# Seven of eight tiles first, decays behind the results, weight sums around the scan: four edits to a scan and feed-forward kernel

## Chip, cores and metric

The kernel runs on one NeuronCore of a Trainium2 chip. The metric is device time of one execution in microseconds (us). Five engines run their own instruction streams in order: TensorE (PE, with its weight loads listed as PEld), VectorE (DVE), ScalarE (ACT), GpSimd (POOL) and SyncE (SP), which here issues every DMA. Matrix results land in PSUM, which the tile names `h`, `even`, `odd`, `oa`, `ob` (in `out_units`), `cb`, `y` and `t_ps` stand for.

## What is computed

The first half is a chunked selective scan (Mamba-2 style) over 4 batches, 8 heads, 768 positions; its output, as a matrix of 3072 tokens by 256, goes through a feed-forward layer with 2048 hidden units and a hard-swish.

```python
# scan, per chunk: cum = cumsum(log a)
L = exp(cum[i] - cum[j]) * (i >= j)
y = ((C @ B.T) * L) @ x + (C @ state) * exp(cum)
state = exp(sum(log a)) * state + (B * exp(cum[-1] - cum)).T @ x
# feed-forward on y as (3072, 256)
h = y @ w_in                       # 256 -> 2048
g = h * clip(h + 3, 0, 6) / 6
out = g @ w_out                    # 2048 -> 256
```

## The kernel before

**Blocks.** The sequence is cut in six chunks of 128 positions. Block k is chunk k of all four batches, 512 tokens, and the loop over k computes its feed-forward layer while the scan of chunk c = k + 1 and the decays of chunk k + 2 (`ahead`) are woven in between. Block 0 uses plain products (`mlp_in`, `first_out`) and, during them, still decodes the weights, which arrive as 64-bit numbers.

**First product, blocks 1 to 5.** It is a Strassen-like product (seven half products for eight) in eight steps s = 0 to 7, each giving two hidden tiles, `even` (g tile 2s) and `odd` (2s + 1). A step's parts are `early`, `lead` (of the step after), `last` (of the step before) and `middle`. DVE and ACT copy partial sums into `up`, DVE adds them (L516, L517), ACT takes the ramp (`ramp`, L524), DVE clamps and multiplies (`times_ramp`, L530). In step 7 the ramp of `even` is taken in two halves of 256 columns: the first half before `middle`, the second behind the first unit of the second product.

**Second product, blocks 1 to 5.** `out_units` yields 14 times, one unit of 8 tiles (16 matmuls in the trace, L599) at a time, into four slots of the PSUM banks `oa` and `ob`; it too is of Strassen form. `g_sums` makes its sums of g on POOL (L586), and `weight_sums` and `in_weight_sums` make the sums of the weights on DVE (L568, L472), once, in block 0 (the last one in block 1). Three DVE steps (`u`, `res`, `res`; L630 to L633) then put a half of the result together, and two stores write it.

**The scan.** `turn` transposes B and C of a chunk (PE L343; ACT `bT` L347; DVE `cT` L359 and `csT` L365). `scores` makes C times B (PE `cb` L376), and DVE multiplies the decays by it (`L`, L384). `mix` makes y and the new state (PE `y` L400, L409, L417), `keep` copies them out (ACT `yT` L432, DVE `state` L435, L440). `rows` loads the decays of a chunk (four DMAs into `L`, L247, and eight into `eto`, L253), `conceal` masks them on POOL (L303), `decay` takes their exponent on ACT (L312).

**What sets the order.** The order is written out by hand: each engine runs its instructions in the order in which the program issues them, and the (i, b) cases of block 0 and the step and unit numbers of the later blocks say where the scan's parts go. Buffers matter in two places: `up` and block 0's result tile `ob` (L546, stored by L547) share one tag with two buffers, and `t_ps`, `oa` and `ob` of `out_units` share two PSUM banks.

```python
parts_of[k, s] = up = ffn.tile([P, 2, 2 * P], FP32, name="up", tag="ob", bufs=2)
ob = ffn.tile([P, 2, DM], FP32, name="ob", bufs=2)
```

Of the kernel before, what the change touches and what calls it, by code (L numbers as in the profile page):

```python
# [8 lines left out]
FP32 = mybir.dt.float32  # L9
# [3 lines left out]
AF = mybir.ActivationFunctionType  # L13
ALU = mybir.AluOpType
# [6 lines left out]
def kernel(  # L21
# [23 lines left out]
    nc = tc.nc  # L45
    P = 128
# [3 lines left out]
    NC = S // P  # L50
    TB = NB * P
# [11 lines left out]
    ffn = ctx.enter_context(tc.tile_pool(name="ffn", bufs=1))  # L63
# [39 lines left out]
    def load_w(i):  # L103
# [24 lines left out]
        out=hide, in_=hide, pattern=[[1, P]], compare_op=ALU.is_ge, fill=-1e5, base=0,  # L128
# [9 lines left out]
    half = const.tile([P, 1], FP32, name="half")  # L138
# [304 lines left out]
    gTs, outs = {}, {}  # L443
# [16 lines left out]
    NJ = NF // 2  # L460
# [58 lines left out]
    def last(k, s):  # L519
        half_product(evens[k, s], 1, in_sums[4][s], y_half(k, 1, 1))  # L520

    def ramp(k, f, h, sl=slice(0, TB)):

        nc.scalar.activation(  # L524
            gTs[k][:, f, sl], h.rearrange("p r i -> p (r i)")[:, sl], AF.Relu, bias=half,
            scale=1.0 / 6.0)

    def times_ramp(k, f, h, sl=slice(0, TB)):
        g = gTs[k][:, f, sl]
        nc.vector.scalar_tensor_tensor(  # L530
            out=g, in0=g, scalar=1.0, in1=h.rearrange("p r i -> p (r i)")[:, sl],
            op0=ALU.min, op1=ALU.mult)

    def first_out(b, i):

# [19 lines left out]
    wsums = {}  # L555
# [32 lines left out]
    def out_units(k):  # L588


        def quarter(e, r, t):
            return g_quarter(k, e, r)[:, :, t * P:(t + 1) * P]

        def total(n, t):
            return gsums[k][n][:, :, t * P:(t + 1) * P]

        def unit(bank, slot, lhs, rhs):
            for j in range(NJ):
                nc.tensor.matmul(  # L599
                    out=bank[:, slot], lhsT=lhs[:, j], rhs=rhs[:, j],  # L600
                    start=(j == 0), stop=(j == NJ - 1), skip_group_check=True)

        for t in range(2):
            oa = ps_o.tile([P, 4, P], FP32, name="oa", tag="o")
            if t == 0:
                unit(oa, 0, quarter(0, 0, 0), w4[:, 0, 0])
                yield
                unit(oa, 3, quarter(0, 0, 1), w4[:, 0, 0])
                yield
            unit(oa, 1, quarter(1, 0, t), w4[:, 1, 0])  # L610
            if t == 0:
                x1 = ffn.tile([P, 2, P], FP32, name="x1")
                nc.scalar.copy(out=x1, in_=oa[:, 0:4:3])
            yield
            ob = ps_o.tile([P, 4, P], FP32, name="ob", tag="o")
            unit(ob, 3, quarter(1, 1, t), wsums[4])
            yield
            unit(oa, 2, total(2, t), wsums[2])
            res = ffn.tile([P, 5, P], FP32, name="res", bufs=2)
            nc.vector.tensor_tensor(  # L620
                out=res[:, 0:5:4], in0=oa[:, 1:3],
                in1=x1[:, t:t + 1].to_broadcast([P, 2, P]), op=ALU.add)
            yield
            unit(ob, 2, total(4, t), w4[:, 1, 1])
            yield
            unit(ob, 0, total(1, t), wsums[1])
            yield
            unit(ob, 1, quarter(0, 1, t), wsums[3])
            u = ffn.tile([P, 2, P], FP32, name="u", bufs=2)
            nc.vector.tensor_tensor(  # L630
                out=u, in0=ob[:, 0:2], in1=res[:, 4:5].to_broadcast([P, 2, P]), op=ALU.add)
            nc.vector.tensor_tensor(out=res[:, 1:3], in0=ob[:, 2:4], in1=u, op=ALU.add)
            nc.vector.tensor_tensor(out=res[:, 3], in0=ob[:, 0], in1=u[:, 1], op=ALU.add)  # L633
            for r in range(2):
                r0 = (t + 2 * r) * S + k * P
                nc.sync.dma_start(
                    out=out[r0:r0 + P, :],
                    in_=res[:, 2 * r:2 * r + 2].rearrange("p m c -> p (m c)"))
            yield

    def rows(c):
        for b in range(NB):
            load_decay(c, b)
        load_eto(c)
# [96 lines left out]
    for k in range(NC):  # L741
        gTs[k] = ffn.tile([P, NF, TB], FP32, name="gT")
        c, ahead = k + 1, k + 2
        if k == 0:
            for f in range(NF):
                mlp_in(k, f)
                for i in weave.get(f, []):
                    weights(i, 1)
            load(ahead)
            weights(NP + 1, 1)  # L750
            weights(NP + 3, 1)
            weights(NP + 2, 3)
            sums, sums_in = weight_sums(), in_weight_sums()
            for i in range(NP):
                for b in range(NB):
                    first_out(b, i)
                    if (i, b) == (0, 0):
                        weights(NP + 3, 1)
                        weights(NP + 2, 1)
                        weights(NP + 3, 3)  # L760
                        rows(ahead)
                    elif (i, b) == (1, 0):
                        for _ in sums_in:
                            pass
                    elif (i, b) == (2, 0):
                        turn(c, 0)
                        turn(c, 1)
                        for b_ in range(NB):
                            conceal(ahead, b_)
                    elif (i, b) == (2, 1):  # L770
                        scores(c, (0, 1))
                    elif (i, b) == (2, 2):
                        decay_ends(ahead, 0)
                        next(sums)
                        next(sums)
                    elif (i, b) == (2, 3):
                        results(c, 0)
                        scores(c, (2, 3))
                        decay_ends(ahead, 1)
                    elif (i, b) == (3, 0):  # L780
                        next(sums)
                        decay_ends(ahead, 2)
                    elif (i, b) == (3, 1):
                        results(c, 1)
                        sum_y(c)
                        rows(ahead + 1)
                        decay_ends(ahead, 3)
                        from_start(ahead)
                    elif (i, b) == (3, 2):
                        lead(c, 0)  # L790
            continue
        for s in range(NJ):
            early(k, s)
            if s == 0:
                if ahead < NC:
                    load(ahead)
                if c < NC:
                    carry(c)
            if s < NJ - 1:
                lead(k, s + 1)  # L800
            elif c < NC:
                turn(c, 1)
            if s:
                last(k, s - 1)
                ramp(k, 2 * s - 2, evens[k, s - 1])
            if s == NJ - 1:
                sl = slice(0, 2 * P)
                ramp(k, 2 * s, evens[k, s], sl)
                times_ramp(k, 2 * s, evens[k, s], sl)
            middle(k, s)  # L810
            if s:
                times_ramp(k, 2 * s - 2, evens[k, s - 1])
            ramp(k, 2 * s + 1, odds[k, s])
            times_ramp(k, 2 * s + 1, odds[k, s])
            if s in (1, 3) and ahead < NC:
                conceal(ahead, s - 1)
                conceal(ahead, s)
            if s == 4 and c < NC:
                turn(c, 0)
            if s in (2, 4, 6):  # L820
                g_sums(k, s - 2)
        for i, _ in enumerate(out_units(k)):
            if i == 0:
                s, sl = NJ - 1, slice(2 * P, TB)
# [52 lines left out]
```

## Time and profile before

| | us |
|---|---|
| median of 3 runs (390.64 to 394.83) | 391.48 |
| the profiled execution | 390.89 |
| its span | 389.2 |
| PE busy | 365.7 (94%) |
| PE weight loads | 310.7 (80%) |
| DVE busy | 229.1 (59%) |
| ACT busy | 188.2 (48%) |
| POOL busy | 132.6 (34%) |
| one block of 1 to 4, start to start | about 58 |

The profile is of one execution. A row of the timeline reads: start, length, engine, line, instruction, tile written <- tiles read, sizes, count; in brackets the idle time before it and what ended that. "SPq" is the queue of SyncE. Line numbers are those of the kernel before. Matmuls are pipelined, so that the length of a group of them is a little more than the time until the next group starts. A `half_product` is x2 and a unit x16 in the trace.

### The profile page before, as it was taken

What the parts mean: (1) busy time and instruction counts of PE and PEld (TensorE: products, weight loads), DVE (VectorE), ACT (ScalarE), POOL (GpSimd) and SP (SyncE); (2) the same over time, 40 slices, a digit from 0 to 9 for tenths busy, and PEclk for the clock granted to TensorE, in tenths of its full rate; (3) what the DMA queues carried; (4) which work ended last, traced back from release to release, by engine and by line L of the source; (5) the groups of instructions that cost most, each with busy time, mean ns of one, the idle gap of its engine ahead of it and who ended that gap; (6) DMA issues with size and microseconds to landing.
All of it is one profiled execution on the core that took longest, in us unless ns stands there. A gap on an engine that the chain in (4) does not pass through costs nothing.

```text
span 389.2 us, 7304 instructions
## 1 busy us (share of the span) xinstructions
PE 365.7 (94%) x2916; PEld 310.7 (80%) x2916; DVE 229.1 (59%) x454; ACT 188.2 (48%) x405; POOL 132.6 (34%) x131
## 2 busy tenths in 40 slices
PE   7889999899499999999999999999998999998995
PEld 4554458678388899987899987999987999987995
DVE  7768999874278733288533388533388523387211
ACT  5759786347267291277290277290276100366100
POOL 1100000533039822149812049800047800058700
PEclk9999999989999999999999999999999999999999
DMA  9949979506880005590004590000000000000000
GB/s 162 237 175 102 306 175 127 198 2 199 140 68 1 2 3 172 148 89 0 2 3 183 139 87 0 2 2 29 29 0 2 2 2 29 27 2 0 3 27 29
DMA packets 86403, 28.18 MB, mean 72 GB/s; under 512 B 75425, under 2 KB 81217, under 8 KB 86369
## 3 DMA queue, kind: packets, MB, share of 16 engines
q1 hardware_dynamic: 86368, 27.71, 35.9%
q8 instruction: 23, 0.38, 0.4%
q14 instruction: 12, 0.09, 0.1%
HBM read 24.48 MB, written 3.23 MB: 71 GB/s over the span
## 4 chain that ended last, share of the span: by engine, by line
PE 68%; DVE 12%; DMA 8%; ACT 7%; SPq 3%; issue 1%; DVEq 0%; ACTq 0%
PE ob L599 19%; PE oa L599 14%; PE even L490 12%; PE odd L490 9%; DMA L<-cum_d 5%; PE cb L376 4%; DVE gT L530 3%; PE y L409 3%; ACT gT L524 2%; PE o L541 2%; DVE odd L517 2%; PE y L400 2%; DVE up L504 1%; SPq L85 1%; DMA raw<-in_moe_w_in_dram 1%
## 5 line engine op out<-in xcount | busy, mean ns | idle before, releaser
L586 POOL TENSOR_TENSOR s<-gT 128x512 f32<-128x512 f32 x20 | 26.3, 1315 | 121.0 <-DVE gT L530 121.0
L490 PE MATMUL even<-ts,w_sum 128*128 128x256 f32 x160 | 48.6, 385 | 6.5 <-DVE gT L530 6.5
L524 ACT ACTIVATE gT<-odd,half 128x512 f32<-128x512 f32 x40 | 27.5, 687 | 46.5 <-DVE odd L517 46.5
L503 ACT COPY even<-odd 128x512 f32<-128x512 f32 x40 | 23.0, 575 | 42.9 <-PE odd L490 40.9
L490 PE MATMUL odd<-yT,w_in 128*128 128x256 f32 x160 | 41.1, 379 | 0.0
L490 PEld LDWEIGHTS even<-ts,w_sum 128*128 128x128 f32 x160 | 30.3, 192 | 12.5 <-DVE gT L530 8.5
L599 PEld LDWEIGHTS oa<-w_out,gT 128*128 128x128 f32 x320 | 38.2, 192 | 2.3 <-issue 1.5
L599 PE MATMUL oa<-w_out,gT 128*128 128x128 f32 x320 | 39.8, 278 | 0.0
L312 ACT ACTIVATE L<-L,cum_n 128x128 f32<-128x128 f32 x128 | 38.4, 392 | 2.9 <-POOL L L303 2.9
L504 DVE COPY up<-odd 128x256 f32<-128x256 f32 x40 | 16.9, 423 | 38.6 <-ACT even L503 29.2
L599 PE MATMUL ob<-t,gT 128*128 128x128 f32 x320 | 39.0, 275 | 0.0
L599 PEld LDWEIGHTS ob<-t,gT 128*128 128x128 f32 x320 | 37.6, 192 | 0.2
L599 PE MATMUL ob<-w_out,s 128*128 128x128 f32 x320 | 37.8, 276 | 0.0
L599 PEld LDWEIGHTS ob<-w_out,s 128*128 128x128 f32 x320 | 36.5, 192 | 1.3 <-issue 1.3
L384 DVE TENSOR_TENSOR L<-L,cb 128x512 f32<-128x512 f32 (+1 forms) x56 | 30.3, 605 | 10.9 <-PE cb L376 10.9
L530 DVE SCALAR_TENSOR_TENSOR gT<-gT,odd 128x512 f32<-128x512 f32 x40 | 27.5, 687 | 10.0 <-ACT gT L524 10.0
L490 PEld LDWEIGHTS odd<-yT,w_in 128*128 128x128 f32 x160 | 30.1, 190 | 3.9
L524 ACT ACTIVATE gT<-even,half 128x512 f32<-128x512 f32 (+1 forms) x45 | 28.6, 649 | 5.5 <-PE even L490 5.5
L530 DVE SCALAR_TENSOR_TENSOR gT<-gT,even 128x512 f32<-128x512 f32 (+1 forms) x45 | 27.9, 619 | 5.0 <-ACT gT L524 5.0
L541 PE MATMUL o<-w_out,gT 128*128 128x256 f32 x128 | 30.6, 397 | 0.0
L490 PE MATMUL even<-yT,w_sum 128*128 128x256 f32 x80 | 24.6, 389 | 5.7 <-DVE odd L517 5.7
L541 PEld LDWEIGHTS o<-w_out,gT 128*128 128x128 f32 x128 | 25.1, 199 | 4.8 <-issue 0.9
(105 smaller groups left out, 616.6 us busy)
## 6 DMA issues: line engine op xcount, KB each, us to landing
L<-cum_d SPq DMA_DIRECT2D x16, 512.0 KB, 6.1
raw<-in_moe_w_in_dram SPq DMA_DIRECT2D x4, 1024.0 KB, 8.5
raw<-in_moe_w_out_dram SPq DMA_DIRECT2D x4, 1024.0 KB, 7.2
xt<-in_x_dram SPq DMA_DIRECT2D x6, 512.0 KB, 8.6
out_dram<-res SPq DMA_DIRECT2D x20, 128.0 KB, 1.8
bc<-in_C_dram SPq DMA_DIRECT2D x6, 256.0 KB, 5.7
bc<-in_B_dram SPq DMA_DIRECT2D x6, 256.0 KB, 8.1
eto<-cum_d SPq DMA_DIRECT2D x40, 32.0 KB, 5.0
```

The costliest lines, as they stand in the source:

```text
L312: nc.scalar.activation(L[:, h], L[:, h], AF.Exp, bias=cum_n[:, c, g:g + 1])
L376: nc.tensor.matmul(out=cbs[q][:, b % 2].rearrange("j h i -> j (h i)"), lhsT=bT[rows, b % 2], rhs=cT[rows, b % 2].rearrange("n t i -> n (t ...
L384: nc.vector.tensor_tensor(out=L[:, :, hs], in0=L[:, :, hs], in1=cbs[q][:, in_pair], op=ALU.mult)
L409: nc.tensor.matmul(out=y_ps[u][32 * q:32 * q + 32, b % 2], lhsT=xt[:, b * NH + h], rhs=L[:, h], start=(c == 0), stop=True, tile_position=( ...
L490: nc.tensor.matmul(out=bank[:, r], lhsT=lhsT, rhs=rhs, start=start, stop=True, skip_group_check=True)
L503: nc.scalar.copy(out=even, in_=odd[:, 1:2].to_broadcast([P, 2, 2 * P]))
L504: nc.vector.tensor_copy(out=up[:, 1], in_=odd[:, 0])
L524: nc.scalar.activation(gTs[k][:, f, sl], h.rearrange("p r i -> p (r i)")[:, sl], AF.Relu, bias=half, scale=1.0 / 6.0)
L530: nc.vector.scalar_tensor_tensor(out=g, in0=g, scalar=1.0, in1=h.rearrange("p r i -> p (r i)")[:, sl], op0=ALU.min, op1=ALU.mult)
L541: nc.tensor.matmul(out=o[:, b % 2], lhsT=gTs[0][:, f, b * P:(b + 1) * P], rhs=w_out[:, f], start=(f == 0 and b % 2 == 0), stop=True, skip_ ...
L586: nc.gpsimd.tensor_tensor(out=o, in0=p_, in1=q_, op=op)
L599: nc.tensor.matmul(out=bank[:, slot], lhsT=lhs[:, j], rhs=rhs[:, j], start=(j == 0), stop=(j == NJ - 1), skip_group_check=True)
```

## The change

It has four parts, all of them in the order or the slicing of the work; the number of matmuls is the same.

1. **Block 0's stores.** `rows(ahead + 1)` moves from the case (3, 1) to behind block 0's loop, so that SP issues the two stores of `ob` before the twelve decay loads of chunk 3.
2. **Weight sums of the first product.** `in_weight_sums` yields after four of its eight sums; the first four stay at (1, 0), the other four move to (2, 1), behind the first `scores` of the scan.
3. **Start of the second product.** The first two units run seven of their eight tiles, and the eighth tile of both (g tile 14) follows behind the third unit; the ramp of g tile 14 is taken whole, in `out_units`' first pause, instead of in halves. The turns of the scan go behind steps 3 and 5 instead of behind step 4 and into step 7; the first `scores` goes one unit later.
4. **The last sum.** For the second half of a block's result, `u` and one `res` step are done one unit earlier, and the last unit goes to a slot of `oa`, so that one step of 256 columns is left behind it.

```diff
-        def unit(bank, slot, lhs, rhs):
-            for j in range(NJ):
+        def unit(bank, slot, lhs, rhs, js=range(NJ), clear=False):
+            for j in js:
...
-                    start=(j == 0), stop=(j == NJ - 1), skip_group_check=True)
+                    start=(clear and j == 0), stop=True, skip_group_check=True)
...
-                unit(oa, 0, quarter(0, 0, 0), w4[:, 0, 0])
+                most, rest = range(NJ - 1), range(NJ - 1, NJ)
+                unit(oa, 0, quarter(0, 0, 0), w4[:, 0, 0], most, clear=True)
                 yield
-                unit(oa, 3, quarter(0, 0, 1), w4[:, 0, 0])
+                unit(oa, 3, quarter(0, 0, 1), w4[:, 0, 0], most)
                 yield
-            unit(oa, 1, quarter(1, 0, t), w4[:, 1, 0])
+            unit(oa, 1, quarter(1, 0, t), w4[:, 1, 0], clear=(t == 1))
             if t == 0:
+                unit(oa, 0, quarter(0, 0, 0), w4[:, 0, 0], rest)
+                unit(oa, 3, quarter(0, 0, 1), w4[:, 0, 0], rest)
...
-            unit(ob, 3, quarter(1, 1, t), wsums[4])
+            unit(ob, 3 - 3 * t, quarter(1, 1, t), wsums[4], clear=True)
...
-            unit(ob, 0, total(1, t), wsums[1])
+            unit(ob, 3 * t, total(1, t), wsums[1])
+            u = ffn.tile([P, 2, P], FP32, name="u", bufs=2)
+            u2 = res[:, 4:5].to_broadcast([P, 2, P])
+            if t:
+                nc.vector.tensor_tensor(out=u, in0=ob[:, 0:4:3], in1=u2, op=ALU.add)
+                nc.vector.tensor_tensor(out=res[:, 1], in0=ob[:, 2], in1=u[:, 1], op=ALU.add)
             yield
-            unit(ob, 1, quarter(0, 1, t), wsums[3])
...
+            if t:
+                unit(oa, 0, quarter(0, 1, t), wsums[3], clear=True)
+                nc.vector.tensor_tensor(
+                    out=res[:, 2:4], in0=oa[:, 0:1].to_broadcast([P, 2, P]), in1=u, op=ALU.add)
+            else:
+                unit(ob, 1, quarter(0, 1, t), wsums[3])
...
                     elif (i, b) == (1, 0):
-                        for _ in sums_in:
-                            pass
+                        next(sums_in)
...
                     elif (i, b) == (2, 1):
                         scores(c, (0, 1))
+                        next(sums_in)
...
                         sum_y(c)
-                        rows(ahead + 1)
...
+            rows(ahead + 1)
             continue
...
-            elif c < NC:
-                turn(c, 1)
...
-            if s == NJ - 1:
-                sl = slice(0, 2 * P)
-                ramp(k, 2 * s, evens[k, s], sl)
-                times_ramp(k, 2 * s, evens[k, s], sl)
...
-            if s == 4 and c < NC:
-                turn(c, 0)
+            if s in (3, 5) and c < NC:
+                turn(c, s // 4)
...
-                ramp(k, 2 * s, evens[k, s], sl)
-                times_ramp(k, 2 * s, evens[k, s], sl)
+                ramp(k, 2 * s, evens[k, s])
+                times_ramp(k, 2 * s, evens[k, s])
...
-                if i in (1, 4):
+                if i in (2, 4):
```

SP, from the first decay loads of the loop on: `L` and `eto` are the decays that `rows` loads, `out_dram<-ob` are block 0's two stores, `bc` and `xt` the inputs of chunk 3. Before:

```order
L247 DMA L<-cum_d 128x1024 x4
L253 DMA eto<-cum_d 16x4x128 x8
L547 DMA out_dram<-ob 128x2x256
L247 DMA L<-cum_d 128x1024 x4
L253 DMA eto<-cum_d 16x4x128 x8
L547 DMA out_dram<-ob 128x2x256
L85 DMA bc<-in_C_dram 128x32x16
```

And with the change:

```order
L247 DMA L<-cum_d 128x1024 x4
L253 DMA eto<-cum_d 16x4x128 x8
L546 DMA out_dram<-ob 128x2x256 x2
L247 DMA L<-cum_d 128x1024 x4
L253 DMA eto<-cum_d 16x4x128 x8
L85 DMA bc<-in_C_dram 128x32x16
```

The second store has moved ahead of the twelve decay loads of chunk 3. DVE, in block 0 around the scan of chunk 1 (`w_sum` and `w_in` are the weight sums of the first product, `t` those of the second). Before:

```order
L472 TENSOR_TENSOR w_in<-w_in 128x4x128
L472 TENSOR_TENSOR w_sum<-w_in 128x512
L472 TENSOR_TENSOR w_sum<-w_sum,w_in 128x512
L472 TENSOR_TENSOR w_sum<-w_in,w_sum 128x512
L472 TENSOR_TENSOR w_in<-w_in 128x4x128
L365 TENSOR_TENSOR csT<-t_ps,eto 128x256 x2
L384 TENSOR_TENSOR L<-L,cb 128x2x256 x4
```

And with the change:

```order
L472 TENSOR_TENSOR w_in<-w_in 128x4x128
L365 TENSOR_TENSOR csT<-t_ps,eto 128x256 x2
L384 TENSOR_TENSOR L<-L,cb 128x2x256 x4
L472 TENSOR_TENSOR w_sum<-w_in 128x512
L472 TENSOR_TENSOR w_sum<-w_sum,w_in 128x512
L472 TENSOR_TENSOR w_sum<-w_in,w_sum 128x512
L472 TENSOR_TENSOR w_in<-w_in 128x4x128
```

Six instructions of the scan stand ahead of the second four sums instead of behind them. PE, from step 7 of the first product into the second product (block 1; a row here is a matmul, of which the trace shows two). Before:

```order
L490 MATMUL even<-yT,w_in 128x256
L490 MATMUL even<-ts,w_sum 128x256
L343 MATMUL t_ps<-ident,bc 128x128 x4
L490 MATMUL even<-yT,w_sum 128x256
L490 MATMUL odd<-ts,w_in 128x256
L490 MATMUL even<-ts,w_sum 128x256
L599 MATMUL oa<-w_out,gT 128x128 x8
L490 MATMUL even<-yT,w_sum 128x256
L599 MATMUL oa<-w_out,gT 128x128 x8
L376 MATMUL cb<-cT,bT 128x256 x8
L599 MATMUL oa<-w_out,gT 128x128 x8
```

And with the change:

```order
L490 MATMUL even<-yT,w_in 128x256
L490 MATMUL even<-ts,w_sum 128x256
L490 MATMUL even<-yT,w_sum 128x256
L490 MATMUL odd<-ts,w_in 128x256
L490 MATMUL even<-ts,w_sum 128x256
L599 MATMUL oa<-w_out,gT 128x128 x7
L490 MATMUL even<-yT,w_sum 128x256
L599 MATMUL oa<-w_out,gT 128x128 x17
L376 MATMUL cb<-cT,bT 128x256 x8
```

The transposes are gone from step 7, the first unit is one tile shorter, and the scores stand behind the third unit and the two single tiles.

More of the change, by code (lines that the diff above doesn't have):

```diff
@@ L520, in last, with ramp, times_ramp @@
         half_product(evens[k, s], 1, in_sums[4][s], y_half(k, 1, 1))
-    def ramp(k, f, h, sl=slice(0, TB)):
+    def ramp(k, f, h):
         nc.scalar.activation(
[L525 to L529, printed above, removed]
+            gTs[k][:, f], h.rearrange("p r i -> p (r i)"), AF.Relu, bias=half, scale=1.0 / 6.0)
+    def times_ramp(k, f, h):
+        g = gTs[k][:, f]
         nc.vector.scalar_tensor_tensor(
-            out=g, in0=g, scalar=1.0, in1=h.rearrange("p r i -> p (r i)")[:, sl],
-            op0=ALU.min, op1=ALU.mult)
+            out=g, in0=g, scalar=1.0, in1=h.rearrange("p r i -> p (r i)"), op0=ALU.min,
+            op1=ALU.mult)
     def first_out(b, i):
@@ L625, in out_units @@
             yield
-            unit(ob, 0, total(1, t), wsums[1])
-            yield
-            unit(ob, 1, quarter(0, 1, t), wsums[3])
[L629 to L633, printed above, removed]
+            unit(ob, 3 * t, total(1, t), wsums[1])
[4 more added lines that the diff above has]
+                nc.vector.tensor_tensor(out=res[:, 1], in0=ob[:, 2], in1=u[:, 1], op=ALU.add)
+            yield
+            if t:
[4 more added lines that the diff above has]
+                unit(ob, 1, quarter(0, 1, t), wsums[3])
+                nc.vector.tensor_tensor(out=u, in0=ob[:, 0:2], in1=u2, op=ALU.add)
+                nc.vector.tensor_tensor(out=res[:, 1:3], in0=ob[:, 2:4], in1=u, op=ALU.add)
+                nc.vector.tensor_tensor(out=res[:, 3], in0=ob[:, 0], in1=u[:, 1], op=ALU.add)
             for r in range(2):
@@ L823 @@
             if i == 0:
-                s, sl = NJ - 1, slice(2 * P, TB)
+                s = NJ - 1
                 last(k, s)
-                ramp(k, 2 * s, evens[k, s], sl)
-                times_ramp(k, 2 * s, evens[k, s], sl)
+                ramp(k, 2 * s, evens[k, s])
+                times_ramp(k, 2 * s, evens[k, s])
                 g_sums(k, s - 1)
```

## The prediction

> **What bounds the kernel now.** I read the page first: TensorE (PE) is busy in 94% of the span, so a gain has to come from the few places where PE stands still, or from those where it runs at a lower clock. The list of PE's waits names the places (line waited on, total us, times, longest):
>
> ```profile
> PE even L490 <- DVE gT L530: 6.5, 5, 1.5
> PE even L490 <- DVE odd L517: 5.7, 1, 5.7
> PE cb L376 <- DVE csT L365: 1.4, 1, 1.4
> ```
>
> The windows give the clock there (stretch, length, busy time of PE, PEld, DVE, ACT, POOL, then granted clock):
>
> ```profile
> 75.60:82.40 6.80, 6.77 (x32) 5.13 (x32) 5.89 (x7) 2.45 (x8) 5.81 (x6) 0.75 0.00 0
> 105.40:109.20 3.80, 3.79 (x11) 3.10 (x12) 2.36 (x5) 2.40 (x5) 0.00 (x0) 0.59 1.36 90
> 241.60:245.00 3.40, 2.16 (x14) 1.68 (x13) 2.95 (x7) 1.65 (x5) 3.32 (x3) 1.00 0.00 0
> ```
>
> So there are two unlike kinds of wait. After the 1.4 and the 5.7 us waits the clock falls to 0.75 and 0.59 of full in the stretch behind: 6.80 x 0.25 = 1.7 us and 3.80 x 0.41 = 1.6 us more, spent inside "busy" time. After the wait that comes once in each of blocks 1 to 5 the clock stays at 1.00. The change touches all three rows, and the end of the kernel.
>
> **Part 1: decays stored behind block 0's results.** The timeline at block 0's end:
>
> ```profile
> 92.54 8.79 SPq L253 DMA_DIRECT2D eto<-cum_d  x8
> 95.41 0.59 ACT L546 COPY ob<-o 128x512 f32<-128x512 f32 x1 [0.55 <-ACT even L503]
> 101.44 0.40 SPq L547 DMA_DIRECT2D out_dram<-ob  x1
> 104.06 0.42 DVE L504 COPY up<-odd 128x256 f32<-128x256 f32 x1 [8.74 <-DMA out_dram<-ob]
> 105.42 1.22 PE L490 MATMUL even<-yT,w_sum 128*128 128x256 f32 x2 [5.71 <-DVE odd L517]
> ```
>
> The second result tile `ob` is ready at 95.41 + 0.59 = 96.00, but SP, which issues in order, is in the decay loads of `rows` until 101.33, so the store leaves at 101.44. `up` has the same two buffers as `ob`, so VectorE (DVE) waits for that store, and PE for DVE. With both stores ahead of `rows`, the store can leave at about 96.05, 5.4 us earlier, and everything behind it follows: PE's wait of 5.71 falls to some 0.3, and the 1.6 us of low clock goes with it. **7.0 us**; between 5.4 (clock dip stays) and 7.3. What is moved pays elsewhere: the four L and eight eto loads, and SP's next loads of bc and xt, start about 5 us later against the clock. Their first reader is POOL's `conceal` in block 1's steps 1 and 3, ahead of `g_sums` on POOL; even 5 us behind the 101.33 at which they now end is about the time of block 1's third step, and the first PE unit that needs a POOL sum is a whole first product later. I cost that at nothing.
>
> **Part 2: weight sums split around the scan.** The same view for block 0's scan of chunk 1, with the grouped row of the sums (its starts 69.1 and 71.8 are those of the first and of the fifth sum):
>
> ```profile
> L472 DVE TENSOR_TENSOR w_sum<-w_in x2: 682/682/682, 69.1 to 71.8; 128x512 f32<-128x512 f32 x2
> 71.73 0.63 ACT L315 ACTIVATE eto<-eto 128x512 f32<-128x512 f32 x1
> 72.52 1.09 DVE L472 TENSOR_TENSOR w_sum<-w_sum,w_in 128x512 f32<-128x512 f32 x1
> 73.22 0.87 ACT L356 ACTIVATE cT<-t_ps,parity 128x256 f32<-128x256 f32 x2
> 73.52 0.70 PE L376 MATMUL cb<-cT,bT 32*128 32x256 f32 x4
> 75.17 0.74 DVE L365 TENSOR_TENSOR csT<-t_ps,eto 128x256 f32<-128x256 f32 x2
> 75.63 1.46 PE L376 MATMUL cb<-cT,bT 32*128 32x256 f32 x12 [1.42 <-DVE csT L365]
> 75.84 4.22 POOL L303 TENSOR_SCALAR_AFFINE_SELECT L<-L 128x1024 f32<-128x1024 f32 x4
> 77.02 5.41 PE L541 MATMUL o<-w_out,gT 128*128 128x256 f32 x16
> 79.18 1.96 DVE L568 TENSOR_TENSOR t<-w_out 128x1024 f32<-128x1024 f32 x1
> 81.18 1.32 DVE L568 TENSOR_TENSOR t<-t,w_out 128x1024 f32<-128x1024 f32 x1
> 84.73 0.29 DVE L435 TENSOR_TENSOR state<-y,parity 128x128 f32<-128x128 f32 x1 [2.23 <-ACT yT L432]
> 85.26 3.72 PE L541 MATMUL o<-w_out,gT 128*128 128x256 f32 x16
> 85.42 2.48 DVE L384 TENSOR_TENSOR L<-L,cb 128x512 f32<-128x512 f32 x4
> 89.51 0.75 PE L409 MATMUL y<-L,xt 128*32 128x128 f32 x20
> ```
>
> Now all eight sums run ahead of csT, so that csT, ready to start when eto is (71.73 + 0.63 = 72.4), starts at 75.17, and the scores stop in the middle. With four sums ahead DVE is free at about 71.9, csT is done by 73.2, and the scores, from 73.52, wait only for the last cT (73.22 + 0.87 = 74.1). They end near 74.8 in place of 77.1: 2.3 us. The 16 matmuls behind them then take the 3.72 of the later, same group in place of 5.41: 1.7 us. PE alone would be 3.7 to 4.0 us ahead at the second `mix` (89.51 would be about 85.7).
> DVE does not follow so far. It multiplies L from about 74.7 to 77.2 (2.48); then come the other four sums, 4 x 0.68 = 2.7 undisturbed to about 3.5 as now beside POOL (the 1.09 row), then the two w_out sums, 1.32 to 1.96 each, 2.6 to 3.3; then two state steps, 0.6; then the second L multiply, 2.5. Ends: 85.6 to 87.1, against 87.9 now. So the second `mix` waits between nothing and 1.4 us; I take 1.0, near the disturbed end, because POOL's four selections now meet these sums. Were each of the four stretched as the 1.96 row is over the 1.32 one (0.64), they would take 5.3, and the wait would be 3.2. Gain: **2.7 us**, between 0.7 and 3.9.
>
> The DVE sum of 1.96 us beside POOL's selection shows the price. The Trainium skill ("SBUF — State Buffer", section SBUF: two separate sides) says that a DVE instruction with two SBUF inputs and a GpSimd one that reads SBUF take one port pair as an exclusive lock, the loser waiting for the whole instruction. The trace agrees in direction. By that rule the four sums would alternate with what is left of the selections; I estimate a gain of 1.0 to 2.6 from it.
>
> **Part 3: seven of eight tiles, the scan's turn earlier, no half ramps.** The boundary in block 3 (the other four are alike):
>
> ```profile
> 241.97 1.08 ACT L524 ACTIVATE gT<-even,half 128x512 f32<-128x512 f32 x2
> 242.19 0.68 DVE L359 TENSOR_TENSOR cT<-t_ps,parity 128x512 f32<-128x512 f32 x1
> 243.12 0.41 DVE L530 SCALAR_TENSOR_TENSOR gT<-gT,even 128x256 f32<-128x256 f32 x1
> 243.59 0.70 PE L490 MATMUL even<-ts,w_sum 128*128 128x256 f32 x2 [1.24 <-DVE gT L530]
> 244.12 1.99 PE L599 MATMUL oa<-w_out,gT 128*128 128x128 f32 x16
> 244.33 0.43 DVE L517 TENSOR_TENSOR odd<-even,up 128x256 f32<-128x256 f32 x1 [0.45 <-PE even L490]
> 244.67 0.68 DVE L530 SCALAR_TENSOR_TENSOR gT<-gT,even 128x512 f32<-128x512 f32 x1
> ```
>
> PE's last `even` product waits for the half ramp, which sits on DVE behind the turn's cT. Both are taken from there: 6.5 us of waits in five blocks. What is late next: tile 12 of g, the seventh in the first unit. It is done at 244.67 + 0.68 = 245.35, and PE comes to it at 244.12 + 6/8 of 1.99 = 245.6, its weights a little sooner. With the wait gone DVE must do the ramps of step 6, L516, L517 and this one without the pause, so I charge 0.2 us a block for a wait there or on ACT's copy of `up`: bounds 0 and 1.24 (the wait simply moves). The eighth tile (g 14) comes after 7 + 7 + 8 tiles and one product, some 5 us behind the last `even`; its chain (product 0.7, ramp below 1.08, multiply 0.68) takes about half of that. **5.5 us**, bounds 0.3 and 6.5. The scores, one unit later, still have two units of 16 matmuls (1.99 in the row of oa) behind them for a 2.48 us multiply. The two single-tile pieces add no matmul.
> The turn now falls on steps 3 and 5 in place of 4 and 7. What a turn does to a step is seen at step 4 (L517 once a step):
>
> ```profile
> 233.91 0.43 DVE L517 TENSOR_TENSOR odd<-even,up 128x256 f32<-128x256 f32 x1
> 237.50 0.43 DVE L517 TENSOR_TENSOR odd<-even,up 128x256 f32<-128x256 f32 x1
> 240.40 0.43 DVE L517 TENSOR_TENSOR odd<-even,up 128x256 f32<-128x256 f32 x1
> ```
>
> 3.59 and then 2.90 us: the step grows by PE's four transposes and DVE has caught up within one step. Two such steps, two apart, cost nothing more.
>
> **Part 4: the last sum.** At the end stand
>
> ```profile
> 385.02 0.42 DVE L630 TENSOR_TENSOR u<-ob,res 128x256 f32<-128x256 f32 x1 [4.93 <-PE ob L599]
> 385.48 0.42 DVE L632 TENSOR_TENSOR res<-ob,u 128x256 f32<-128x256 f32 x1
> 385.82 0.28 DVE L633 TENSOR_TENSOR res<-ob,u 128x128 f32<-128x128 f32 x1
> 385.93 0.81 SPq L636 DMA_DIRECT2D out_dram<-res  x2
> ```
>
> Three steps become one of 0.42, so the last store can be issued at about 385.5; the first store is issued a unit earlier, and the last no longer stands behind it (0.81 for two). The last leaves some 0.4 + 0.4 us earlier: **0.9 us**, between 0.4 and 1.2.
>
> **Sum.** 7.0 + 2.7 + 5.5 + 0.9 = 16.1 us. The profiled execution took 390.89 us, so 374.8; the median of before is 391.48, 0.6 above it, which gives 375.4.
>
> **The rivals.**
> 1. *The boundary wait only moves* (to tile 12, or to ACT's copy). For it: DVE's five instructions of a step (two like L530, L517, two like L504) come to 2.6 us in a step of 2.9 to 3.0, and tile 12 arrives just in time. Against: the rows above. Part 3 then gives nothing: 375.4 + 5.5 = 380.9.
> 2. *The scan's gain is lost on DVE or by the clock.* The second `mix` waits 3.2 in place of 1.0, and the clock falls behind that wait as it does behind the 1.42 us one: 2.2 + 1.6 lost, 379.2. For it: POOL's selections lie there.
> 3. *The dip at 75.60 to 82.40 isn't caused by the wait.* Then 16 matmuls stay at 5.41, 1.7 us lost, of which DVE's lag hides 1.0: 376.1. Against: the same group at 85.26 behind no wait takes 3.72; the five 1.24 us waits leave the clock at 1.00, which speaks for it. The Trainium skill ("TensorE: Matmul & The Clock Gate", Part 1) has the clock fall after about 3.4 us of idle; by that rule a 1.42 us gap isn't enough, and the row of 0.75 speaks against it unless the scores, on 32 rows, count as idle too.
> 4. *Slower.* The first unit, started at once, stands at tile 12 so long that the clock gate trips in each of five blocks. The price is 1.6 us of low clock per block on top of the wait; to pass 395.4 (1% above) from rival 1's 380.9 it needs 14.5 / 5 = 2.9 a block, so a wait of 1.24 + 1.3 = 2.5 us there. DVE would have to be 2.5 us late; the L517 rows show it back in step after one step.
> 5. *It does little:* two of the three waits stay because something else ends them at the same time, within 1% (387.6 to 395.4; a measurement of this kernel can't tell less). It needs 12 of 16 us lost.
>
> Chances: forecast 0.60 (371.5 to 378), rival 1 0.14, rival 2 0.10, rival 3 0.08, rival 5 0.05, rival 4 0.03. The best bounds together (7.3 + 3.9 + 6.5 + 1.2 = 18.9) give 372.6, and 371.5 leaves about a us for the median; upward the range, 371.5 to 381.5, takes in rivals 1 to 3, each of whose own times is unsure by a few us. Faster by over 1%: 0.92; same 0.05; slower 0.03.
>
> **What would show it.** Part 1: no DVE wait on the store of ob above 1.5 us, no PE wait of 5 us, no stretch at 0.59 behind it. Part 2: csT before 73.5, granted clock 1.00 behind the scores, and a PE wait in the second `mix` below 1.4. Part 3: the row of five waits on gT L530 gone, each of the five blocks shorter by about 1.1 us. Part 4: one DVE step behind the last matmul. A new wait of over 1 us in every block, in oa or in even, would make the prediction wrong.

## The result, and the profile after

The changed kernel takes 374.97 us (median of 4 runs, 373.86 to 376.12), against 391.06 us for the kernel before in the same comparison: a ratio of 0.957, 95% interval 0.950 to 0.965. A second comparison with more runs (375.17 against 391.96) gave 0.956, 0.954 to 0.959. The forecast was 375.4 us. The profiled execution took 375.2 us, with a span of 373.5. One execution of one kernel below (the exponent of `eto` earlier) took 2105.66 us, for a reason that no trace shows, and is left out of that kernel's median.

PE's list of waits in the changed kernel (line waited on, us in total, times, longest) has lost the row of five waits on the half ramp and that of the 5.7 us behind the store, and the one on csT has shrunk from 1.4 to 0.3:

```profile
PE d L281 <- POOL head L145: 1.9, 1, 1.9
PE cb L376 <- ACT bT L347: 0.8, 1, 0.8
PE y L409 <- DVE state L435: 0.8, 1, 0.8
PE cb L376 <- DVE csT L365: 0.3, 1, 0.3
```

The page's first part shows PE at 98% of the span:

```profile
PE 365.0 (98%) x2916; PEld 309.3 (83%) x2916; DVE 228.6 (61%) x449; ACT 187.3 (50%) x400; POOL 131.7 (35%) x131
```

The windows that answer to the two low-clock rows of before (75.60 to 82.40 and the stretch behind block 1's first wait) show the granted clock, the number behind the five engines, at 1.00 in both:

```profile
75.60:82.40 6.80, 6.78 (x94) 5.45 (x98) 5.89 (x9) 2.55 (x9) 4.95 (x5) 1.00 0.03 7
97.80:101.60 3.80, 3.77 (x17) 3.02 (x18) 2.74 (x6) 3.04 (x7) 2.09 (x2) 1.00 1.00 387
```

The executions don't start alike. In the first 70 us, where nothing was changed, PE's first products ran at half speed for a while in some of them, and the transposes of chunk 1, which begin the stretch that was changed, came at 70.82 us before and at 71.84 us after; over all profiles below they lie between 70.75 and 73.33. I therefore compare the stretch from those transposes to the end of the span. It took 318.38 us before and 301.66 us after (301.67 in a second profile of the changed kernel): 16.7 us less, against a forecast of 16.1.

Block 0's end in the timeline of the changed kernel:

```profile
93.47 0.58 ACT L545 COPY ob<-o 128x512 f32<-128x512 f32 x1 [0.57 <-ACT even L503]
94.65 1.80 SPq L247 DMA_DIRECT2D L<-cum_d  x4
96.47 0.42 DVE L504 COPY up<-odd 128x256 f32<-128x256 f32 x1 [3.11 <-DMA out_dram<-ob]
96.74 1.03 PE L490 MATMUL odd<-yT,w_in 128*128 128x256 f32 x4
97.83 0.70 PE L490 MATMUL even<-yT,w_sum 128*128 128x256 f32 x2
```

DVE still waits for the store of `ob`, but 3.11 us in place of 8.74 (a run below, where it doesn't wait for the store, has it idle for 2.38 us here anyway), and PE goes on about 0.2 us late behind the four matmuls ahead.

The scan of chunk 1:

```profile
74.14 0.42 DVE L365 TENSOR_TENSOR csT<-t_ps,eto 128x256 f32<-128x256 f32 x1 [1.24 <-ACT cT L356]
75.14 0.42 DVE L365 TENSOR_TENSOR csT<-t_ps,eto 128x256 f32<-128x256 f32 x1 [0.58 <-ACT cT L356]
75.62 1.13 PE L376 MATMUL cb<-cT,bT 32*128 32x256 f32 x10 [0.31 <-DVE csT L365]
76.68 3.72 PE L540 MATMUL o<-w_out,gT 128*128 128x256 f32 x16
78.84 1.45 DVE L472 TENSOR_TENSOR w_sum<-w_in 128x512 f32<-128x512 f32 x1
85.28 2.47 DVE L384 TENSOR_TENSOR L<-L,cb 128x512 f32<-128x512 f32 x4
87.48 1.17 PE L409 MATMUL y<-L,xt 128*32 128x128 f32 x32
```

The 16 matmuls behind the scores take 3.72 us (5.41 before). csT now waits for ACT's cT, a wait that the prediction didn't have: csT doesn't read cT, but both read the tile `t_ps`. The first of the four sums behind the scan is stretched from 0.68 to 1.45 us beside POOL's selections, and the second multiply still ends in time: `mix` at 87.48 is about 0.1 us longer than the 1.08 us one in the scan's first half.

The boundary in block 2:

```profile
173.40 0.70 PE L490 MATMUL even<-yT,w_sum 128*128 128x256 f32 x2
173.93 0.59 PE L490 MATMUL odd<-ts,w_in 128*128 128x256 f32 x2
174.38 0.70 PE L490 MATMUL even<-ts,w_sum 128*128 128x256 f32 x2
174.91 1.88 PE L599 MATMUL oa<-w_out,gT 128*128 128x128 f32 x14
175.57 0.68 DVE L529 SCALAR_TENSOR_TENSOR gT<-gT,even 128x512 f32<-128x512 f32 x1
176.63 0.60 PE L490 MATMUL even<-yT,w_sum 128*128 128x256 f32 x2
```

No row carries a wait in brackets, yet small ones are left: elsewhere one product follows another in 0.43 us, here in 0.53 twice, and the 14 matmuls of the seven tiles take 176.63 - 174.91 = 1.72 us, where 16 take 1.79 in the units behind. From one block's first unit to the next one's are 57.02 us now and 58.07 before (58.34 from block 3's to block 4's); in the last interval 55.58 against 56.88.

And the end:

```profile
368.35 1.95 PE L599 MATMUL oa<-t,gT 128*128 128x128 f32 x16
369.01 0.29 DVE L635 TENSOR_TENSOR res<-ob,u 128x128 f32<-128x128 f32 x1
370.34 0.42 DVE L640 TENSOR_TENSOR res<-oa,u 128x256 f32<-128x256 f32 x1 [1.03 <-PE oa L599]
```

From the start of the first DVE step behind the last unit to the end of the span: 373.5 - 370.34 = 3.2 us, before 389.2 - 385.02 = 4.2.

### The profile page after: what moved, and what is told of

Its sections match the earlier page's. It is cut to its first block, busy times and chain, and to the rows that moved or that the text cites. A ratio compares the mean times of both kernels' runs of the same rounds, so it can differ in the third digit from the quotient of the medians.

```text
span 373.5 us, 7300 instructions
## 1 busy us (share of the span) xinstructions
PE 365.0 (98%) x2916; PEld 309.3 (83%) x2916; DVE 228.6 (61%) x449; ACT 187.3 (50%) x400; POOL 131.7 (35%) x131
## 4 chain that ended last, share of the span: by engine, by line
PE 94%; ACT 1%; DVE 1%; DMA 1%; issue 1%; DVEq 0%; ACTq 0%
PE even L490 19%; PE ob L599 17%; PE oa L599 17%; PE odd L490 13%; PE h L448 7%; PE o L540 7%; PE cb L376 4%; PE y L409 3%; PE y L400 2%; PE d L289 1%; PE t_ps L343 1%; PE d L292 1%; PE y L417 1%; DMA out_dram<-ob 1%; DMA pre<-in_a_dram 1%; PE d L281 1%
## 5 line engine op out<-in xcount | busy, mean ns | idle before, releaser
L524 ACT ACTIVATE gT<-even,half 128x512 f32<-128x512 f32 x40 | 27.7, 694 | 4.4 <-PE even L490 4.4
L529 DVE SCALAR_TENSOR_TENSOR gT<-gT,even 128x512 f32<-128x512 f32 x40 | 27.2, 679 | 4.4 <-ACT gT L524 4.4
L599 PE MATMUL ob<-t,gT 128*128 128x128 f32 x240 | 29.7, 277 | 0.0
L599 PEld LDWEIGHTS ob<-t,gT 128*128 128x128 f32 x240 | 28.0, 192 | 1.3 <-issue 1.3
L540 PE MATMUL o<-w_out,gT 128*128 128x256 f32 x128 | 28.9, 381 | 0.0
L448 PE MATMUL h<-yT,w_in 128*128 128x512 f32 x64 | 27.7, 594 | 0.6 <-ACT yT L432 0.6
L540 PEld LDWEIGHTS o<-w_out,gT 128*128 128x128 f32 x128 | 24.0, 190 | 4.3 <-issue 1.1
```

The source lines that it names most:

```text
L448: nc.tensor.matmul(out=h.rearrange("p r i -> p (r i)"), lhsT=w_in[:, j, f * P:(f + 1) * P], rhs=yTs[k][:, j].rearrange("p b i -> p (b i)") ...
L524: nc.scalar.activation(gTs[k][:, f], h.rearrange("p r i -> p (r i)"), AF.Relu, bias=half, scale=1.0 / 6.0)
L529: nc.vector.scalar_tensor_tensor(out=g, in0=g, scalar=1.0, in1=h.rearrange("p r i -> p (r i)"), op0=ALU.min, op1=ALU.mult)
L540: nc.tensor.matmul(out=o[:, b % 2], lhsT=gTs[0][:, f, b * P:(b + 1) * P], rhs=w_out[:, f], start=(f == 0 and b % 2 == 0), stop=True, skip_ ...
L599: nc.tensor.matmul(out=bank[:, slot], lhsT=lhs[:, j], rhs=rhs[:, j], start=(clear and j == 0), stop=True, skip_group_check=True)
```

## The experiments

**Undoing each part alone.** Four kernels are the changed one with one part put back. Part 1:

```diff
                         sum_y(c)
+                        rows(ahead + 1)
...
-            rows(ahead + 1)
             continue
```

> The changed kernel with the decay loads of chunk 3 back ahead of the second store of block 0. My theory: the store waits in SP's order behind the loads again, DVE waits for it some 8 us, PE 5 to 6 us, and the clock falls behind it; the profile's span is 6.5 to 7.5 us longer than the changed kernel's (near 380.5). Rival (the gain of the changed kernel comes mostly from the five boundaries, the store was only the excuse of a wait that something else ends): under 3 us longer, and another wait in the place of the one on the store.

Measured: 382.88 us (ratio to before 0.973, 0.969 to 0.978); from the transposes to the end 309.89 us, 8.2 more than the changed kernel, and 7.9 of them between the second `mix` and block 1's first unit. The other 0.3 us lie between block 3's first unit and block 4's (57.38 us), the interval that was long in the kernel before too; why isn't shown. The waits and the clock are back (the timeline of this kernel, then its windows):

```profile
101.39 0.42 DVE L504 COPY up<-odd 128x256 f32<-128x256 f32 x1 [8.67 <-DMA out_dram<-ob]
102.75 1.22 PE L490 MATMUL even<-yT,w_sum 128*128 128x256 f32 x2 [5.61 <-DVE odd L517]
```

```profile
101.05:104.47 3.42, 1.72 (x4) 1.45 (x5) 2.16 (x5) 1.74 (x4) 0.00 (x0) 0.50 1.47 104
104.47:107.88 3.41, 3.41 (x9) 2.69 (x9) 2.29 (x5) 1.36 (x3) 0.00 (x0) 0.50 1.60 114
```

The same in the kernel before, whose wait ran from 99.71 to 105.42:

```profile
98.28:101.69 3.41, 1.43 (x7) 0.92 (x5) 0.00 (x0) 0.00 (x0) 0.00 (x0) 1.00 0.32 88
105.11:108.52 3.41, 3.10 (x7) 2.52 (x8) 1.93 (x5) 2.05 (x4) 0.00 (x0) 0.50 1.39 85
```

The mechanism is the one forecast; the size is 1 us above it, because PE works longer at the low clock here: (1.72 + 3.41) x 0.5 = 2.6 us lost to it, 3.10 x 0.5 = 1.6 in the kernel before. The waits are nearly the same (5.61 and 5.71 us), but the clock goes down and up only at borders that lie 3.41 us apart in these traces (the two falls of the kernel before, at 77.80 and 105.11, are eight such clock steps apart). Before, it fell 0.31 us ahead of PE's return and rose one clock step later; here it fell 1.70 us ahead, and the clock step in which PE came back, half of it idle, was followed by a second low one. The rival that the boundaries make most of the gain falls.

Part 2:

```diff
-                        next(sums_in)
+                        for _ in sums_in:
+                            pass
...
                         scores(c, (0, 1))
-                        next(sums_in)
```

> The changed kernel with all eight weight sums ahead of the scan again. My theory: PE waits about 1.4 us in the scores of block 0, the 16 matmuls behind them run at a granted clock near 0.5 for part of the time (5.4 us in place of 3.7), and the second mix comes 3.0 us later, so the span is about 3 us longer. Rival (the dip of the clock in the kernel before had another cause than that wait): the wait comes back, the dip doesn't, and the span is 1.0 to 1.4 us longer.

Measured: 377.80 us (0.962, 0.957 to 0.967); from the transposes to the end 304.67, 3.0 us more than the changed kernel, all of it by the second `mix`. The two rows of the kernel before are back to the hundredth:

```profile
75.65 1.46 PE L376 MATMUL cb<-cT,bT 32*128 32x256 f32 x12 [1.42 <-DVE csT L365]
77.03 5.41 PE L540 MATMUL o<-w_out,gT 128*128 128x256 f32 x16
```

So the dip comes and goes with the wait.

Part 3 (with the half ramps, the place of the turns and of the first scores, as in the kernel before):

```diff
-                unit(oa, 0, quarter(0, 0, 0), w4[:, 0, 0], most, clear=True)
+                unit(oa, 0, quarter(0, 0, 0), w4[:, 0, 0], clear=True)
...
+            if s == NJ - 1:
+                sl = slice(0, 2 * P)
+                ramp(k, 2 * s, evens[k, s], sl)
+                times_ramp(k, 2 * s, evens[k, s], sl)
...
-                if i in (2, 4):
+                if i in (1, 4):
```

> The changed kernel with the second product's start, the half ramps, the place of the turns and of the first scores as before. My theory: five waits of about 1.24 us on the half ramp come back and the small new ones (0.4 us a block) go, so 1.05 us a block, 5.3 us longer in all. Rival (PE's waits at the boundary are hidden or replaced in the changed kernel by as much elsewhere in the block): under 2 us longer.

Measured: 380.56 us (0.968, 0.964 to 0.973); from the transposes to the end 307.12, 5.5 us more. The block distances are 58.06 to 58.08 and 56.88 again, and PE's list has its row back:

```profile
PE even L490 <- DVE gT L530: 6.2, 5, 1.3
```

Part 4:

```diff
-            unit(ob, 3 - 3 * t, quarter(1, 1, t), wsums[4], clear=True)
+            unit(ob, 3, quarter(1, 1, t), wsums[4], clear=True)
...
-            unit(ob, 3 * t, total(1, t), wsums[1])
+            unit(ob, 0, total(1, t), wsums[1])
...
-            if t:
...
-            else:
+            if True:
```

> The changed kernel with the three result steps behind the last unit again. My theory: only the end of the last block moves, 0.9 to 1.0 us longer from the last matmul to the end of the span, and nothing in blocks 1 to 4. Rival (the three DVE steps also hold up DVE at the start of the next block): another 0.2 us or more for each of four blocks, 1.8 us in all.

Measured: 375.11 us (0.956, 0.951 to 0.961), which the runs can't tell from the changed kernel; from the transposes to the end 302.65, 1.0 us more, with block distances of 57.02 and 57.03. Only the end moves.

The four together make 8.2 + 3.0 + 5.5 + 1.0 = 17.7 us, 1.0 more than the whole change gained: that much is the longer low clock of the first. Taken the other way round, the stretch from the second `mix` to block 1's first unit was 39.06 us before and is 32.17 with parts 1, 2 and 4 in, so part 1 is worth 6.9 us, and 6.9 + 3.0 + 5.5 + 1.0 = 16.4; the other 0.3 is the long interval of the kernel before.

**How the late store reaches PE.** The kernel before, with a buffer for `ob` alone:

```diff
-            ob = ffn.tile([P, 2, DM], FP32, name="ob", bufs=2)
+            ob = ffn.tile([P, 2, DM], FP32, name="ob", tag="ob_own", bufs=1)
```

> The kernel before with one edit: block 0's result tile ob has a buffer of its own and shares none with up; the decay loads stay ahead of the second store. My theory (the wait goes from the late store to PE only through the shared buffer): the store still leaves some 5 us late, but DVE doesn't wait for it, PE's wait of 5.7 us and the low clock behind it are gone, and the span is 6.5 to 7.5 us shorter than the kernel before's. Rival (the decay loads themselves hold PE up, by their traffic or by data that block 1 needs): under 2 us shorter.

Measured: 384.12 us (0.979, 0.975 to 0.982); from the transposes to the end 310.61, 7.8 us less than before. The store is as late as ever, and nobody waits for it:

```profile
96.48 0.59 ACT L546 COPY ob<-o 128x512 f32<-128x512 f32 x1 [0.55 <-ACT even L503]
98.76 0.42 DVE L504 COPY up<-odd 128x256 f32<-128x256 f32 x1 [2.38 <-ACT even L503]
102.53 0.40 SPq L547 DMA_DIRECT2D out_dram<-ob  x1
```

The chain is the shared buffer, not the traffic. From the second `mix` to the first unit it takes 31.57 us, 0.6 less than the reordering (32.17), since not even the store's own 2.6 us (101.44 to 104.06 in the kernel before) are waited for. Both together weren't tried.

**What the turn's place is worth.**

```diff
             if s < NJ - 1:
                 lead(k, s + 1)
+            elif c < NC:
+                turn(c, 1)
...
-            if s in (3, 5) and c < NC:
-                turn(c, s // 4)
+            if s == 4 and c < NC:
+                turn(c, 0)
```

> The changed kernel with the scan's turns back at step 4 and in step 7, all else as changed. My theory (DVE is the engine that the second product's start waits for): cT and csT put about 1.0 us of DVE work ahead of tile 12, the transposes give 0.4 back, and each of blocks 1 to 4 gets 0.3 to 0.6 us longer (57.3 to 57.6 from start to start in place of 57.02), block 5 stays; 1.2 to 2.4 us in all. Rival (the seven tiles and the whole ramp are all that counts): under 0.1 us a block.

Measured: 376.98 us (0.960, 0.955 to 0.964); 303.24 from the transposes to the end, 1.6 us more, and block distances of 57.39 to 57.40, 0.37 above 57.02, with 56.29 in place of 55.58 in the last. The wait is where it was looked for, at the seventh tile (PE's list of waits, then the timeline):

```profile
PE oa L599 <- DVE gT L529: 2.4, 4, 0.6
```

```profile
177.51 0.68 DVE L529 SCALAR_TENSOR_TENSOR gT<-gT,even 128x512 f32<-128x512 f32 x1
178.24 0.49 PE L599 MATMUL oa<-w_out,gT 128*128 128x128 f32 x2 [0.60 <-DVE gT L529]
```

So about 1.6 us of part 3's 5.5 are due to the turn's place. The rest belongs to the whole ramp, the seven tiles and the later scores together, which no run takes apart.

**Which wait lowers the clock.** Copies on DVE ahead of csT in block 0 lengthen PE's wait in the scores.

```diff
+        if c == 1 and p == 0:
+            dummy = ffn.tile([P, 2 * P], FP32, name="dummy")
+            for _ in range(4):
+                nc.vector.tensor_copy(out=dummy, in_=t_ps[:, 0:2].rearrange("p j i -> p (j i)"))
         if c:
```

> The changed kernel with four idle DVE copies of 128x256 (their result is used by nobody) ahead of csT in block 0's scan, so that PE waits about 1.0 us in the scores in place of 0.3. Theory that a wait has to reach about 1.4 us there to lower the clock: the 16 matmuls behind the scores keep 3.7 us. Theory that any wait of a us next to the 32-row scores lowers it: 5 us or more.

> As the run with four copies, with eight, so that PE waits about 2.4 us in the scores. Theory that the wait lowers the clock: the 16 matmuls take 5.4 us, or the scores and they together lose 1.6 us beyond the wait. Rival (the dip belongs to what DVE and POOL do at that time, not to PE's wait): 3.7 us.

With four copies (376.32 us, one run) PE waits 1.18 us and the 16 matmuls keep their time; with eight (380.74 us, one run) it waits 3.01 us, and the scores and the matmuls behind them both run slow. The timeline of each, first four, then eight:

```profile
76.24 1.37 PE L380 MATMUL cb<-cT,bT 32*128 32x256 f32 x12 [1.18 <-DVE csT L369]
77.54 3.72 PE L544 MATMUL o<-w_out,gT 128*128 128x256 f32 x16
```

```profile
77.34 2.31 PE L380 MATMUL cb<-cT,bT 32*128 32x256 f32 x12 [3.01 <-DVE csT L369]
79.58 6.05 PE L544 MATMUL o<-w_out,gT 128*128 128x256 f32 x16
```

That any wait of 1 us beside the scores is enough falls, and so does the rival that DVE's or POOL's work makes the dip. The copies, which read only `t_ps`, had to wait for ACT's cT too (1.25 us with four), which points to the shared tile as what puts the two engines in order.

The 1.18 us and the 1.42 us of the undone sums don't make a threshold, though: the waits also differ in where they fall between the clock's borders. In the clock step that ends with the fall in the kernel before (74.39 to 77.80) PE stood still for 1.24 us; with four copies it stood still for 1.18 us in the step from 73.20 to 76.61 (counted from a fall at 18.59 in that trace), nearly as long, and the clock stayed. The start of the kernel, which these changes leave alone, shows it more plainly: there the same wait of 0.84 us and the same sixteen scores ended at half the clock in four of the fourteen profiles (the second run of the changed kernel, the turns back, four copies, both small edits) and at 1.00 in ten. First the run with both small edits (the last below), then the kernel before:

```profile
14.90 2.94 PE L375 MATMUL cb<-cT,bT 32*128 32x256 f32 x16 [0.84 <-ACT bT L347]
17.91:21.33 3.42, 3.42 (x20) 1.59 (x18) 1.44 (x5) 0.60 (x1) 0.00 (x0) 0.50 1.03 412
```

```profile
15.15 2.94 PE L376 MATMUL cb<-cT,bT 32*128 32x256 f32 x16 [0.84 <-ACT bT L347]
16.36:23.19 6.83, 6.62 (x85) 4.46 (x84) 5.12 (x15) 3.50 (x7) 0.41 (x1) 1.00 1.02 408
```

In the first the scores lie inside the clock step that ends with the fall at 17.91; in the second, counting back in steps from 77.80, a border at 16.36 divides them.

**What is left.** Three kernels for small remains, run beside the changed kernel again.

> The changed kernel once more, as the measure for the three beside it: 374 to 376 us; the five block distances within 0.03 us of those of its first profile, and the stretch up to the first weight sum anywhere from 69 to 71.3 us, as in the runs so far.

375.17 us; 301.67 us from the transposes to the end, block distances of 57.02 and 57.03. The stretch before the first weight sum was 71.66 us, a little past what I had expected.

Six tiles first:

```diff
-                most, rest = range(NJ - 1), range(NJ - 1, NJ)
+                most, rest = range(NJ - 2), range(NJ - 2, NJ)
```

> The changed kernel with six of eight tiles in the first two units and two tiles each behind the third. My theory (tile 12 is the one that comes late, by some 0.16 us a block): the first unit runs without a gap, 0.1 to 0.2 us a block shorter, 0.5 to 0.9 us in all. Rival (the loss of 0.4 us a block sits wholly in step 7's products, which wait for L517 and for ACT's copy of up): no change of the block distances.

Measured: 373.49 us (ratio to before 0.952, 0.950 to 0.955), block distances of 56.87 and 55.42, 0.16 less each; 300.86 us from the transposes to the end, 0.8 less. The first unit runs without a gap: its 12 matmuls take 1.34 us up to the next product.

```profile
173.85 1.50 PE L599 MATMUL oa<-w_out,gT 128*128 128x128 f32 x12
175.19 0.60 PE L490 MATMUL even<-yT,w_sum 128*128 128x256 f32 x2
```

Tile 12 was late by that much; the 0.2 us in step 7's own products stay.

The exponent of `eto` earlier:

```diff
-            from_start(c)
             carry(c)
...
+                    elif (i, b) == (1, 2):
+                        from_start(c)
```

> The changed kernel with the exponent of eto (ACT) in block 0 taken three units earlier, in ACT's idle time. My theory (csT, and with it the scores, wait for ACT's run of bT, exponent and cT, not for DVE any more): the scores end 0.3 to 0.5 us earlier, PE's wait of 0.31 is gone, and the second mix comes 0.3 to 0.5 us earlier. Rival (DVE's weight sums set the second mix): the scores end earlier, the second mix doesn't.

Measured: 374.12 us (0.955, 0.952 to 0.958); 301.43 us from the transposes to the end, 0.2 less, and the second `mix` 0.17 us earlier. That is a miss: ACT's cT is ready sooner, but POOL's work, which waits for the same exponent, comes forward too and stretches DVE's sums ahead of csT. The last of them, beside POOL's selections, takes 1.58 us in place of 0.69:

```profile
72.78 5.13 POOL L303 TENSOR_SCALAR_AFFINE_SELECT L<-L 128x1024 f32<-128x1024 f32 x4
73.29 1.58 DVE L471 TENSOR_TENSOR w_in<-w_in 128x512 f32<-128x512 f32 x1
```

> Both of the two edits together. If both theories hold, 0.8 to 1.4 us less than the changed kernel from the first weight sum to the end; if both rivals hold, nothing.

Both: 374.06 us (0.953, 0.950 to 0.955); 300.56 us from the transposes to the end, 1.1 less than the changed kernel. By that stretch it is the shortest of all; in the medians it can't be told from the six tiles alone (373.49), and both lie 1 to 2 us below the changed kernel's 375.17.

## Why the prediction was right, by its own steps

**Part 1** (7.0 forecast, 6.9 measured). The wait through SP's order and the shared buffer, and the clock's fall behind it, were both as forecast; a buffer of its own (384.12 us) shows the first, the granted clock of 1.00 from 97.80 the second. DVE was then late by the store's own time, which cost PE about 0.2 us at once and as much again in the step behind. That the later decay loads cost nothing held: POOL's selections waited for them 15.8 us in all in place of 8.3, and behind the first 2 us PE waited for nothing of POOL's. One sign set for this part failed: DVE's wait on the store was to stay under 1.5 us and was 3.11, since the store itself takes over 2 us to come through; that cost little because DVE would have been idle for 2.38 anyway.

**Part 2** (2.7 forecast, 3.0 measured) has the right size by luck, with two errors that cancel. The scores were to end 2.3 us earlier; relative to the transposes they ended 1.4 us earlier, since csT waits behind ACT's cT, and I had only looked at when `eto` and DVE were free; the sign of csT before 73.5 wasn't met either (74.14 and 75.14, in an execution that started 1.0 us later). The clock's 1.7 us came as forecast. The wait of 1.0 us in the second `mix`, charged for DVE's lag, didn't come (0.1). My stretched sums were 3.5 us; they took 1.45 + 0.78 + 0.69 + 0.68 = 3.6, but the two w_out sums behind them no longer met POOL and took 1.2 each, below the 1.32 that I had taken as the lower bound. POOL's selections and DVE's sums in the timeline of the changed kernel:

```profile
75.51 4.23 POOL L303 TENSOR_SCALAR_AFFINE_SELECT L<-L 128x1024 f32<-128x1024 f32 x4
```

```profile
80.32 0.78 DVE L472 TENSOR_TENSOR w_sum<-w_sum,w_in 128x512 f32<-128x512 f32 x1
81.14 0.69 DVE L472 TENSOR_TENSOR w_sum<-w_in,w_sum 128x512 f32<-128x512 f32 x1
81.75 0.68 DVE L472 TENSOR_TENSOR w_in<-w_in 128x512 f32<-128x512 f32 x1
82.35 1.22 DVE L567 TENSOR_TENSOR t<-w_out 128x1024 f32<-128x1024 f32 x1
```

The first sum, stretched to 1.45 us, ended at 78.84 + 1.45 = 80.29 us, and the selections at 75.51 + 4.23 = 79.74; the three sums behind ran almost free. That agrees roughly with the Trainium skill ("SBUF — State Buffer", section SBUF: two separate sides), by which such an instruction waits until the GpSimd one is through: 79.74 and the 0.68 us of a free sum would end at 80.42.

**Part 3** (5.5 forecast, 5.5 measured). The term was right, its two halves were both too small: without the change a block loses not 1.24 but about 1.45 us (58.07 - 57.02 + 0.4), and with it 0.4, not 0.2: about 0.2 in step 7's products, which follow L517 and ACT's copy of `up` too closely, and 0.16 at tile 12. The turns at steps 3 and 5 cost nothing that shows.

**Part 4** (0.9 forecast, 1.0 measured) held.

**The rivals.** The wait that only moves (1) is there, but at a quarter of its size. The loss on DVE (2), the slow case (4) and the small one (5) didn't come. That the dip isn't caused by the wait (3) is refuted by the undone sums and the eight copies. The Trainium skill ("TensorE: Matmul & The Clock Gate", Part 1) asks for about 3.4 us of idle time; by that rule the 1.42 us wait would have left the clock alone, and the measurement says otherwise. What the page says of a window of 3413 ns that runs freely agrees with the low-clock stretches of part 1, of one clock step of 3.41 us in the kernel before and two in the kernel with the loads put back: 1.6 and 2.6 us lost for nearly the same wait (5.71 and 5.61).

The median agrees with the forecast within 0.4 us, and that closeness is partly luck: the changed stretch gained 0.6 us more than forecast, and the profiled execution reached it 1.0 us later than that of the kernel before.

## What to carry to other kernels

A wait of PE has a second price in the granted clock of the stretch behind it: read that number in windows behind each wait before the wait is called small. The price isn't fixed by the wait's length: nearly the same wait cost 1.6 and 2.6 us here. Where a store holds up an engine through a shared buffer, either its place in the issuing queue or the buffer can be changed, and the buffer was worth 0.6 us more. When a wait is removed, look for every engine that reads the same tile, not only for the one that the trace names: the next one was 0.3 us behind.

## What the runs showed of the hardware

At one place, with the same 32-row scores around it, a wait of 1.42 us brought the clock to one half for 3.41 us in each of three kernels (16 matmuls in 5.41 us for 3.72), and one of 1.18 us, in a single run, left it at 1.00. Fifteen waits of 1.23 to 1.50 us between full matmuls, five in each of three kernels, didn't lower it, nor did 1.98 us of standing still in the clock step from 98.28 to 101.69. A low stretch lasted one clock step of 3.41 us or two. The place of a wait between the clock's borders counts (the start: same wait, four falls in fourteen), and the comparison with the full matmuls suggests that the 32-row ones count for less; how the two are weighed no run here shows.

DVE's sums of two SBUF tiles of 128x512 took 0.68 us alone, 1.45 and 1.58 us at most beside POOL's selections, and 0.78 to 1.09 beside its products, while the multiply by `cb`, with one input in PSUM, took 2.48 us for four in both surroundings.
